# A fused Nyström attention and MLP on one core: batch 0's attention rebuilt step by step, paired x tiles, and the order of the steps written out

## The chip, the cores and the metric

The kernel runs on one core of a Trainium2 chip. The time is device microseconds of one execution, and of several executions the median is given. The core has five engines that run side by side and wait for one another by semaphores: TensorE (PE, with its weight loads listed apart as PEld), VectorE (DVE), ScalarE (ACT), GpSimd (POOL) and SyncE (SP, which issues the DMAs).

## The reference

q, k and v are [8 batches, 8 heads, 576 positions, 64], x has 512 channels, the hidden layer 2048.

```python
q_lm = q.reshape(B, H, 32, 18, D).mean(axis=3)      # 32 landmarks, k_lm likewise
A, Bm, C = sm(q, k_lm), sm(q_lm, k_lm), sm(q_lm, k) # softmax(scale * a @ b.T)
Z = Bm.T / (norm1(Bm) * norminf(Bm) + 1e-6)
for _ in range(6):
    Z = 2 * Z - Z @ Bm @ Z
x = (A @ Z @ C @ v).transpose(0, 2, 1, 3).reshape(B, S, 512)
xn = (x - mean(x)) / sqrt(var(x) + 1e-6) * g_ln
out = x + relu(xn @ w_ch1) @ w_ch2
```

## The kernel before, in words

**Attention.** A batch has two units of four heads (u = 0, 1). For each the kernel loads q, k and v, casts them to fp16 (`nat`), turns them over (`xT`), sums them to landmarks (`lm`), and forms the three exponentials: `psb` (landmarks by landmarks), `psc` (by k, into `ect`) and `psa` (q by landmarks, into `ea`). The softmax of `psb` (`softmax_of`, L756, with `rsum` and `rcr`) and its gram matrix (`gram_of`, L797, with `csum` and `cinv`) give the start `st` of the inverse. `iterate` (L817) is one of six steps: eight 32x32 products on PE into a bank, then one scalar_tensor_tensor on DVE that writes the new `st`. Between the steps stand other matmuls: `pscv`, the product of `ect` with v, whose scaled copy is `cv`, and `psd`, the divisors of `ea`, from which ACT makes `lns`. After the last step, `pszt` and `pszc` are the products of the inverse with `cv`, and `zt` and `zcbd` their copies. `ea` is multiplied by `lns`.

**First layer.** x isn't multiplied by w1. For each batch, m = zt·w1 is formed instead (`products`, `copies`), in four quarters f of 512 columns, and a chunk (128 of the 2048 hidden columns, 16 to a batch) is `psh` = m·ea: eight matmuls of 288 columns, then relu to `hT`. w1 is scaled by g when it comes (`scale_w1`, by POOL or ACT). The mean of x is taken out by the column means of w1: four matmuls per quarter with the constant `lesser` (`less_mean`, L1393), copied to `less` by `copy_mean`; `copies` adds less times `zsum` to m. Later `center_w1` takes the mean out of w1 itself.

**Second layer and x.** x itself comes block by block, 36 blocks of 128 positions, as zcbd·ea, into tiles `xblk` (twelve of [128, 512] in `xpool`); `two_rows` (L857) makes two blocks at once in `psr` and evicts each in two copies of 256 columns. `measure` takes mean and deviation of a block (`six`, `stats`). The second layer is 128x512 matmuls of hT with w2; for late batches some are replaced by seven products of sums (`w2mix`). `finish_block` scales by the deviation, adds x, and the block is stored.

**The order.** `attention0` (L610) is batch 0's attention, a generator written by hand: each `yield` is a point at which the code below `warm(27, 160)` (L1917, the start of the program) issues other work, such as the eight loads of w1 and thirteen of its scales on POOL. `first_layer0` (L1520) is batch 0's first layer with the column means of the quarters 1 to 3 (the mean of quarter 1 before the first chunk, of 2 and 3 after the chunks 2 and 5, the products of a quarter after the chunks 1, 4 and 7). The other batches go in sets (1), (2), (3, 4), (5, 6), (7) through `Coming` (loads, casts, transposes) and `attention2`. From then on `run` (L1888) chooses at every step among five streams: attentions, landmark totals, first layers, batch 0's first rows, second layers. A model, `Clock` (L85), keeps what each engine will be free at; a stream comes next when its operands are there by that model, in the order of the streams, and a table `AFTER` holds some steps back until another stream has come so far. Before each choice `help_out` (L1761) issues the steps beside the streams where an engine is free by the model: loads, casts, jobs of DVE's transposes, measures, centring, mixing of w2. Idle matmuls on zeros (`warm`) stand at the start (27 of 160 columns), after three of the four turned tiles of batch 0 (3 of 256 each) and twice in the softmax and gram (4 and 2 of 256).

The copies of m for one quarter, which the prediction speaks of (before, in `copies`):

```python
n = 2 if (self.b, f) == (0, 0) else 1
for part in range(n):
    cols = ts(part, 512 // n)
    for u, (_, total) in enumerate(self.units):
        dve.scalar_tensor_tensor(out=self.m16[f][:, u, cols], in0=less(f)[:, cols], scalar=total, ...)
    while between:
        between.pop(0)()
```

## Time and profile before

| what | value |
|---|---|
| median of 3 runs | 263.51 us (263.14 to 263.57) |
| span of the profiled execution | 261.4 us |
| PE busy | 252.8 us (97%) |
| DVE, ACT, POOL busy | 209.9, 171.8, 136.8 us |
| moved by DMA | 46.68 MB, of which read 36.70 |
| median before less span | 2.1 us |

The profile is of one execution; its span runs from its first to its last instruction, and what lies around that is in the time of a run. A row of a timeline gives start, duration, engine, line, operation, the written and the read tiles, a count of neighbours put together (then the duration is from the first's start to the last's end), and in brackets the idle time before it with what ended it. In a table by stretches each engine has its busy time with its count of instructions, then follow the granted clock of PE (1.00 is full), the share of the DMA engines and GB/s. Groups give count, total busy time, mean ns of one. Since a helper records each operation, nearly all rows have the helper's line, L312 or L318, and are told apart by tiles.

### The profile page before, as it was taken

Reading aid. Unit: us, or ns where it says so; the run is one execution under the profiler, and the core shown is the slowest. Engines: PE = TensorE matmul, PEld = TensorE weight load, DVE = VectorE, ACT = ScalarE, POOL = GpSimd, SP = SyncE. Lnnn points to the kernel's source line nnn. Section 1 sums busy time; section 2 is a strip of 40 time slices with the busy share of each in tenths; the row PEclk is TensorE's granted clock in tenths of the full one; section 3 lists DMA queues with packets and bytes.
Section 4 is the critical chain, followed back from the end, with each engine's and each line's share of the span. In section 5 each row is a group of like instructions: output and inputs, shape, how many; then the busy total and the mean of one; then the engine's idle time right before and its main releaser. Section 6 shows DMA issues by size and latency. Waiting matters only on the chain.

```text
span 261.4 us, 8559 instructions
## 1 busy us (share of the span) xinstructions
PE 252.8 (97%) x3519; PEld 167.7 (64%) x3519; DVE 209.9 (80%) x480; ACT 171.8 (66%) x332; POOL 136.8 (52%) x162
## 2 busy tenths in 40 slices
PE   7899999999999999999999999999999999999994
PEld 6645754556455574546655466588878875888883
DVE  2767965999979997899996972999399889696862
ACT  2588986458956878489986669634977863766000
POOL 5288779999951889899899955400000014000000
PEclk9999999999999999999999999999999999999999
DMA  6999999999947998669731101110330007100705
GB/s 238 381 393 381 384 391 387 355 251 345 349 145 213 282 375 308 185 158 336 244 84 43 26 21 40 45 38 3 80 84 4 3 11 162 32 3 0 163 19 182
DMA packets 24142, 46.68 MB, mean 179 GB/s; under 512 B 2980, under 2 KB 3240, under 8 KB 24104
## 3 DMA queue, kind: packets, MB, share of 16 engines
q1 hardware_dynamic: 23624, 45.50, 54.5%
q10 hardware_dynamic: 480, 0.66, 0.7%
q8 instruction: 27, 0.44, 0.7%
q14 instruction: 11, 0.09, 0.1%
HBM read 36.70 MB, written 9.44 MB: 177 GB/s over the span
## 4 chain that ended last, share of the span: by engine, by line
PE 82%; DVE 11%; DMA 3%; ACT 2%; issue 1%; SPq 0%; DVEq 0%
PE bank L318 53%; PE psh L318 21%; DMA stg<-in_q_dram 3%; DVE m L312 2%; PE psd L318 2%; PE pscv L318 2%; DVE six L312 1%; DVE xblk L312 1%; DVE w L312 1%; DVE part L312 1%; ACT hT L312 1%; PE psea L318 1%; DVE nat L312 1%; DVE xT L312 1%; PE psec L318 1%
## 5 line engine op out<-in xcount | busy, mean ns | idle before, releaser
L318 PE MATMUL bank<-w,hT 128*128 128x512 f16 (+3 forms) x528 | 109.5, 335 | 0.0
L312 ACT ACTIVATE hT<-psh 128x576 f16<-128x576 f32 x123 | 76.7, 655 | 23.9 <-PE psh L318 22.2
L318 PE MATMUL psh<-ea,m 128*128 128x288 f16 x512 | 79.0, 286 | 0.4 <-DVE ea L312 0.3
L318 PEld LDWEIGHTS <-hT 128*128 128x128 f16 x656 | 60.3, 98 | 29.5 <-issue 4.7
L318 PEld LDWEIGHTS <-m 128*128 128x128 f16 x512 | 49.4, 98 | 19.3 <-issue 2.8
L312 DVE SCALAR_TENSOR_TENSOR xblk<-bank,rstd,xblk 128x256 f32<-128x256 f32 (+2 forms) x77 | 39.2, 543 | 14.8 <-PE bank L318 14.6
L312 POOL TENSOR_TENSOR ea<-ea,lns 128x576 f16<-128x576 f16 x14 | 18.2, 1318 | 53.1 <-ACT lns L312 51.8
L312 POOL CAST nat<-stg 128x1152 f16<-128x1152 f32 x23 | 26.1, 1147 | 11.3 <-DVE xT L312 8.7
L312 DVE BATCH_NORM_STATS2 six<-xblk 128x6 f32<-128x512 f32 x36 | 24.3, 674 | 0.6 <-ACT xblk L312 0.5
L312 POOL CAST natv<-stg 128x1152 f16<-128x1152 f32 (+1 forms) x17 | 19.4, 1166 | 9.4 <-DMA stg<-in_v_dram 7.9
L312 DVE STREAM_TRANSPOSE xT<-nat 128x576 uint32<-128x576 uint32 x28 | 21.2, 759 | 0.0
L318 PE MATMUL bank<-w2mix,hT 128*128 128x256 f16 x128 | 17.7, 273 | 0.0
L318 PE MATMUL bank<-w2mix 128*128 128x256 f16 x128 | 17.4, 273 | 0.0
L312 DVE SCALAR_TENSOR_TENSOR st<-st,bank 128x128 f16<-128x128 f16 (+3 forms) x36 | 13.2, 366 | 5.0 <-PE bank L318 4.8
L312 ACT ACTIVATE lns<-psd 128x576 f32<-128x576 f32 x16 | 10.3, 645 | 7.9 <-PE psd L318 7.7
L312 DVE TENSOR_REDUCE part<-xT 128x32 f16<-128x576 f16 x20 | 14.3, 744 | 0.1
L312 ACT COPY xblk<-bank 128x512 f32<-128x512 f32 (+1 forms) x19 | 11.0, 592 | 4.9 <-PE bank L318 4.8
L312 POOL TENSOR_TENSOR asum<-asum 128x256 f32<-128x256 f32 (+1 forms) x20 | 13.0, 650 | 1.6
L318 PEld LDWEIGHTS <-w2mix 128*128 128x128 f16 x128 | 12.3, 98 | 2.0
L312 ACT ACTIVATE ec<-psec 128x256 f16<-128x256 f32 (+1 forms) x42 | 12.0, 430 | 1.9 <-PE psec L318 1.8
L318 PEld LDWEIGHTS <-st 32*32 32x32 f16 (+1 forms) x380 | 6.5, 90 | 10.5 <-DVE st L312 6.3
L312 POOL TENSOR_TENSOR asum<-nat 128x512 f32<-128x512 f16 x10 | 11.7, 1172 | 1.1 <-ACT nat L312 0.4
(133 smaller groups left out, 375.2 us busy)
## 6 DMA issues: line engine op xcount, KB each, us to landing
stg<-in_q_dram SPq DMA_DIRECT2D x16, 576.0 KB, 6.7
stg<-in_k_dram SPq DMA_DIRECT2D x15, 576.0 KB, 6.0
out_dram<-xblk SPq DMA_DIRECT2D x66, 128.0 KB, 2.4
wstg<-in_moe_w_ch_dram SPq DMA_DIRECT2D x16, 512.0 KB, 7.2
stg<-in_v_dram SPq DMA_DIRECT2D x5, 576.0 KB, 7.7
stg<-in_v_dram SPq DMA_DIRECT2D x40, 72.0 KB, 2.8
stg<-in_v_dram SPq DMA_DIRECT2D x6, 288.0 KB, 5.7
stg<-in_v_dram SPq DMA_DIRECT2D x12, 144.0 KB, 3.1
```

The source lines that it names most:

```text
L312: return lambda *args, **kw: keep(getattr(self.engine, op)(*args, **kw))
L318: keep(nc.tensor.matmul(o, l, r, start=start, stop=stop, tile_position=(rb, cb), skip_group_check=(skip or cb != 0)))
```

## The change

In batch 0: the last k tile is cast in two halves with another order of axes; its turned tile goes partly to a bank and is copied in 512 and 640 columns, the second behind the softmax; the idle matmuls in softmax and gram go, the others become 11 of 384 at the start and 2 of 384 after each of three tiles; the gram has a tile of its own; scores and the divisors are issued unit by unit between the steps; `pscv` is one tile of PSUM's second ring with both units, scaled by one product, one reciprocal and one product; the first quarter's mean is taken after the steps; the `ea` halves 0 go to POOL; `zt` is copied by DVE, unit by unit; the products of the first quarter are issued unit by unit; m comes in 128, 128 and 256 columns for the first quarter and 256 and 256 for the second; `less` comes in 128 and 384. The mean of quarter 1 comes after chunk 1, and the later means and products one chunk later than before. w1's first quarter comes in four DMAs instead of two. Four scales of w1 stand on POOL ahead of the `ea` halves and nine behind.

In all batches: `xpool` holds five pairs [128, 2, 512] and two singles `xone`; `two_rows` evicts in two copies of 512, each on DVE or ACT, whichever the model has free sooner. The choice of the next step, `help_out` and `AFTER` give way to a string `ORDER` that lists the steps: a digit is a stream, a letter a step beside them (J a job, M measure, C centre, X and W mixing, K cast, L load), a number behind it a count. A step that cannot be issued yet is kept in `late` and tried before the next. (The code for sets in `BY_HEAD` and `PAIRED` is added too; both sets are empty.)

```diff
+            for r in range(2) if (nm, u) == ("k", U - 1) else (None,):
...
+                    dve.tensor_copy(out=t[:, :, r, :].rearrange("p j (a d) -> p a j d", a=2),
+                                    in_=raw[nm, u][:, r, :, :].rearrange("p j (a d) -> p a j d", a=2))
...
-    xpool = Ring(name="xpool", bufs=12)
+    xpool = Ring(name="xpool", bufs=5)
...
-        dve.tensor_copy(out=last_tile[0][:], in_=last_tile[1][:])
-        yield "landmarks"
+        t, pst, rest, turn = last_turn
+        dve.tensor_copy(out=t[:, 0:NFIRST, :], in_=pst[:, 0:NFIRST, :])
...
-        st, bmT = softmax_of(psb, W)
-        warm(4, 256)
...
-        cinv, _ = gram_of(p1([P, 4, W * LM], "psse"), st, bmT, W, lambda: warm(2, 256))
...
+        scores_of_q(0)
+        turn(range(NBEFORE, NJ))
+        scores_of_k(0)
+        st, bmT = softmax_of(psb, W)
+        dve.tensor_copy(out=t[:, NFIRST:NJ, :], in_=rest)
+        banks.release(*last_bank)
+        lns = []
+        _, csum = gram_of(p1([P, 4, W * LM], "psse"), st, bmT, W, None, p1([P, 4, W * LM], "gram"))
+        scores_of_q(1)
+        scaled_by_pe()
...
+            if it == 0:
+                scores_of_k(1)
             if it == 1:
+                lns.append(divisors(ea[0]))
+            if it == 2:
                 product(range(NJ // 2))
-            if it == 2:
+            if it == 3:
                 product(range(NJ // 2, NJ))
...
+                dve.tensor_tensor(out=rcv[:], in0=pscv_[0][:, :, D], in1=csum[:], op=ALU.mult)
+                dve.reciprocal(out=rcv[:], in_=rcv[:])
...
+            if it == 4:
+                dve.tensor_tensor(out=cv[:], in0=pscv_[0][:, :, 0:D2],
+                                  in1=rcv[:, :, None].broadcast_to([P, W, D2]), op=ALU.mult)
+                lns.append(divisors(ea[1]))
             if it == 5:
-                less_mean(0, 3, 4, False)
-                scale_ea(0, 0)
+                less_mean(0, 0, 2)
+                scale_ea(dve, 0, 1)
...
+        scale_ea(pool, 0, 0)
+        scale_ea(pool, 1, 0)
...
+        less_mean(0, 2, 4, False)
+        for w in range(W):
+            dve.tensor_copy(out=zt[:, :, w, :], in_=pszt[w][:, :, 0:LM])
+        copy_mean(0)
...
-            copy = sooner(1024, clock.at(t))
-            for i, (j, _) in enumerate(mine):
-                for hp in range(2):
-                    copy(crossed(x_of(j), hp), to[:, hp, i, :, :].rearrange("p u (r d) -> p u r d", r=2))
+            for hp in range(2):
+                sooner(512, clock.at(t))(
+                    crossed(x, hp), to[:, hp, :, :, :].rearrange("p i u (r d) -> p i u r d", r=2))
...
+            for cols in (((ds(0, P), ds(P, P), ds(2 * P, 2 * P)), (ds(0, 256), ds(256, 256)))[f] if self.b == 0 and f < 2
+                         else (ds(0, 512),)):
...
-        less_mean(1)
...
-            if m in (2, 5):
-                f = 2 if m == 2 else 3
+            if m in (1, 3, 6):
+                f = (m + 3) // 3
...
-            if m in (1, 4, 7):
+            if m in (2, 5, 8):
...
+    ORDER = (
+        "2 3 4 215 3 23 M 2 J2 3 22 J3 2 1 3 2 M 22 L J 0 J 2 J 12 L 22 L 1 3 2 0 3 0 43 M 22 "
...
+        for k in order + [None] * 400:
+            settle()
+            late = [x for x in late if not issue(x)]
...
+            elif k in late or not issue(k):
+                late.append(k)
...
-    warm(27, 160)
+    warm(11, 384)
...
-            warm(3, 256)
+            warm(2, 384)
...
     for i in range(8):
         load_w1(i)
+        if i < 2:
+            for c in range(2):
+                scale_w1(i, c, pool)
+    for it in range(7):
+        next(a0)
+    for i in range(2, 8):
         for c in range(2):
-            if i % 2 == 0 or c == 0 or i == 1:
+            if i % 2 == 0 or c == 0:
                 scale_w1(i, c, pool)
```

## The prediction

> **What bounds the kernel now.** I read the page first (busy shares, slices, chain), then the stretches, then the timelines of the opening 25 us, and last the groups by shape.

> ```profile
> PE 252.8 (97%) x3519; PEld 167.7 (64%) x3519; DVE 209.9 (80%) x480; ACT 171.8 (66%) x332; POOL 136.8 (52%) x162
> ...
> PE   7899999999999999999999999999999999999994
> ...
> PEclk9999999999999999999999999999999999999999
> ...
> PE 82%; DVE 11%; DMA 3%; ACT 2%; issue 1%; SPq 0%; DVEq 0%
> ```

> TensorE is busy 97% of 261.4 us and carries 82% of the chain. Only the first two slices and the last show it short of work. So the change can save in two ways: close what is left idle on PE, nearly all of it in the opening, or take away matmul work. The stretches say where the idle time lies (first pair after the stretch: its length and PE's busy time; third: DVE's; then the clock).

> ```profile
> 11.70:14.50 2.80, 2.72 (x77) 1.73 (x77) 2.19 (x9) 1.75 (x4) 2.17 (x2) 1.00 1.01 365
> 18.50:21.40 2.90, 2.28 (x40) 0.98 (x40) 2.54 (x7) 1.95 (x5) 2.78 (x4) 1.00 1.05 386
> 21.40:46.00 24.60, 23.91 (x364) 14.15 (x363) 17.82 (x48) 20.43 (x44) 20.38 (x21) 1.00 1.05 386
> 46.00:70.00 24.00, 23.83 (x241) 13.48 (x245) 23.59 (x48) 16.73 (x33) 22.97 (x25) 1.00 1.00 325
> 70.00:160.00 90.00, 89.82 (x1401) 51.60 (x1374) 78.42 (x173) 68.58 (x137) 71.73 (x74) 1.00 0.61 185
> 160.00:240.00 80.00, 79.94 (x1067) 61.18 (x1065) 64.99 (x149) 54.24 (x103) 9.20 (x7) 1.00 0.16 38
> ```

> PE idles 0.69 us between 21.4 and 46, 0.17 to 70, 0.18 to 160 and 0.06 to 240: 1.1 in all that better cover could close (besides what hides inside the modelled ends of pipelined matmuls). The opening is another matter: 0.62 of the 2.90 from 18.5 on are idle, and before that, "busy" is not useful work: until 18.5 us the 32x32 products and idle matmuls only sit beside a chain of short DVE steps. What sets that stretch is DVE's latency, one step after the other:

> ```profile
> 8.41 2.23 DVE L312 CAST nat<-stg 128x1152 f16<-128x1152 f32 x3 [1.26 <-DMA stg<-in_q_dram]
> ...
> 11.68 0.76 DVE L312 COPY xT<-pst 128x1152 f16<-128x1152 f16 x1 [0.21 <-PE pst L322]
> ...
> 12.43 0.22 DVE L312 TENSOR_REDUCE rsum<-bank 128x2 f32<-128x64 f32 x1
> ...
> 13.80 0.22 DVE L312 TENSOR_REDUCE csum<-bank 128x2 f32<-128x64 f32 x1 [0.42 <-PE bank L318]
> ...
> 14.83 0.29 DVE L312 SCALAR_TENSOR_TENSOR st<-st,bank 128x128 f16<-128x128 f16 x1 [0.35 <-PE bank L318]
> 15.48 0.29 DVE L312 SCALAR_TENSOR_TENSOR st<-st,bank 128x128 f16<-128x128 f16 x1 [0.36 <-PE bank L318]
> ...
> 18.12 0.22 DVE L312 SCALAR_TENSOR_TENSOR st<-st,bank 128x64 f16<-128x64 f16 x1
> ```

> ```profile
> 14.54 0.24 PE L318 MATMUL bank<-st 32*32 32x64 f16 x8
> ...
> 19.67 1.18 PE L318 MATMUL bank<-w,lesser 128*128 128x512 f16 x4
> 20.69 0.41 PE L318 MATMUL psh<-ea,m 128*128 128x288 f16 x2
> 21.38 1.14 PE L318 MATMUL psh<-ea,m 128*128 128x288 f16 x6 [0.28 <-DVE ea L312]
> ```

> The first inverse product starts at 14.54, the last st step ends at 18.34, the first chunk of the first layer (psh) starts at 20.69, and PE runs full from 21.38. From there on an earlier start moves everything behind it, if nothing else is late.

> **The change part by part.** I make the sum against the profiled execution (span 261.4 us; the three timed runs have a median of 263.51, so 2.1 us lie around the span and I leave them unchanged).

> (1) k's last tile is cast in two halves with the short axis outermost. The group rows of the casts, and the transfers of the halves:

> ```profile
> L312 DVE CAST nat<-stg 128x1152 f16<-128x1152 f32 x3 | 2.3, 760 | 5.2 <-DMA stg<-in_q_dram 4.5 <-DMA stg<-in_k_dram 0.7
> ...
> L312 DVE CAST nat<-stg 128x576 f16<-128x576 f32 x2 | 1.5, 754 | 0.0
> ```

> ```profile
> L337 SPq DMA_DIRECT2D stg<-in_k_dram x2: 447/457/467, 2.3 to 2.8; - x2
> ...
> DMA to landing us min/median/max: 6.8/6.9/7.0
> ```

> A half (576) costs as much as a whole (1152): 0.754 against 0.760. The whole walks its two slots outermost, the half its nine. Written as the whole is, a half would take half the whole plus some fixed cost, about 0.40 (my choice); the other bound is the old 0.754, no gain. The second half lands at 2.83 + 7.0 = 9.85 and its cast ends at 10.64 today, so it ends at about 10.29: −0.35. [...]

> (2) Softmax and gram. Today the 0.76 copy of xT stands ahead of rsum, and csum (13.80) waits on PE, where scores and idle matmuls stand ahead of the gram. After: the copy is 512 + 640 with the second behind the softmax, the idle matmuls there go, g's transpose and psc(1) move back, the gram has its own tile. The stages rsum (ready 0.2 sooner without the copy), csum (0.42 of waiting, most of it gone) and (1) add up to −0.9; psa(0), three turns and psc(0) now stand ahead of rsum's products on PE, and I give back 0.15. First inverse product: 14.54 − 0.75 = 13.8 (bounds 13.4 to 14.5, all or nothing).

> (3) The six steps, 0.65 apart (14.83 to 15.48). The same products and exponentials lie between them. New is the scaling of pscv for both units in one operation:

> ```profile
> 16.52 0.23 DVE L312 RECIPROCAL rcv<-bank 128x1 f32<-128x1 f32 x2
> ...
> 16.96 0.41 DVE L312 TENSOR_SCALAR cv<-bank,rcv,cinv 128x130 f16<-128x130 f32 x1
> ```

> ```profile
> L312 DVE TENSOR_TENSOR cv<-pscv,rcv 128x260 f16<-128x260 f32 x3 | 1.3, 428 | 0.1
> ...
> L312 DVE TENSOR_TENSOR rcv<-pscv,csum 128x2 f32<-128x2 f32 x3 | 0.5, 155 | 1.1 <-PE pscv L318 1.1
> ```

> 0.43 replaces 2 x 0.41, but rcv costs 0.16 + 0.17 (product, then reciprocal) where 0.23 was, and the one cv must end before pszt. I charge 0.15: last st ends at 18.34 − 0.75 + 0.15 = 17.75.

> (4) From there to psh. zt goes to DVE, unit by unit; the product of unit 0 comes first; m is written in 128, 128 and 256 columns instead of 256 and 256, `less` in 128 and 384. The chunk's first matmul needs only the first 128 columns of both units, so one m piece of a shorter size, not two of 0.44:

> ```profile
> 19.72 0.88 DVE L312 SCALAR_TENSOR_TENSOR m<-less,zsum,bank 128x256 f16<-128x256 f16 x2
> 20.51 1.19 DVE L312 TENSOR_TENSOR ea<-ea,lns 128x288 f16<-128x288 f16 x2
> ```

> Of four ea halves DVE keeps two (0.54 each by its group); two go to POOL, ahead of nine of its w1 scales. That takes DVE's 1.19 out from between m and psh. First psh: 20.69 − 0.6 − 0.4 = 19.7; the second half of chunk 0, which waits for ea today at 21.38, at about 20.1.

> (5) What is given back. Today's gap isn't empty: the four `lesser` matmuls of w1's second quarter (the row at 19.67) fill it. After the change they follow chunk 1, and two of the first quarter's move out from between the steps to behind pszc. A row of four such matmuls in a full stretch, and a step beside it:

> ```profile
> 40.74 0.24 PE L318 MATMUL bank<-st 32*32 32x64 f16 x8 [0.25 <-DVE st L312]
> 40.91 1.04 PE L318 MATMUL bank<-w,hT 128*128 128x512 f16 x4
> ```

> At about 0.22 each (four, with the last one's tail, in 1.04) the mean's four are 0.9 of work that PE must now do after 20.1, where it used to be free; the first quarter's two still fall into idle time, at most half. So the lead of 1.0 at psh (20.69 to 19.7), and of 1.3 at the second half of chunk 0, shrinks to about 1.3 − 0.9 = **0.4** once chunk 1, that mean and the second product are done. Bounds: −1.0 (the mean's matmuls too find idle time) to 0.

> (6) POOL. Its thirteen w1 scales run unbroken today:

> ```profile
> 16.25 6.60 POOL L312 TENSOR_SCALAR w<-wstg,g_sb 128x512 f16<-128x512 f32 x8 [0.28 <-DMA wstg<-in_moe_w_ch_dram]
> 23.05 2.04 POOL L312 TENSOR_SCALAR w<-wstg,g_sb 128x512 f16<-128x512 f32 x3 [0.21 <-DMA wstg<-in_moe_w_ch_dram]
> 25.84 1.14 POOL L312 CAST nat<-stg 128x1152 f16<-128x1152 f32 x1 [0.75 <-DMA stg<-in_k_dram]
> ```

> After four of them it now waits for unit 1's divisors, whose last exponential is

> ```profile
> 17.77 0.69 ACT L312 ACTIVATE lns<-lns 128x576 f32<-128x576 f32 x1
> ```

> and ends at 18.46 today (about the same after: a step later in the order, 0.6 sooner by (2) and (3)). Then come two ea halves; no row has one on POOL, the nearest are 0.54 on DVE (above) and half of POOL's 1.32 for the whole, so some 0.7 each with DVE's as the lower bound:

> ```profile
> L312 POOL TENSOR_TENSOR ea<-ea,lns 128x576 f16<-128x576 f16 x14 | 18.2, 1318 | 53.1 <-ACT lns L312 51.8
> ```

> The nine scales that follow take 7.4 (6.60 / 8 each; the last three, at 0.68, less) and end at 18.5 + 1.4 + 6.9 = 26 to 27.3 at worst, where the last one ends at 25.09 today; POOL's cast of batch 1's k at 25.84 had 0.75 to spare, so it is 0.2 to 1.5 late. Behind it on POOL stand the three other casts of batch 1, and for them PE's sums and DVE's transposes; but PE has first-layer chunks in plenty there. The second quarter of w1 has two scales on POOL ahead of the mean after chunk 1 (21 to 21.8); they end by 18.5 + 1.4 + 1.6 = 21.5. I cost both at 0; if that cover is gone, PE stands up to 0.6 at that mean, and as much at batch 1's sums.

> (7) SP: two transfers of 512 KB become four of 256, two issues more of 0.457 each (the row of L337), behind the loads of v. Hidden: the queue then waits for stg slots anyway.

> (8) The written order. In batch 1 the softmax now has zcbd's products beside it and st's first wait (0.25 at 40.74) goes, which can give back up to the 0.69 idle of 21.4 to 46; but two inverse steps come together with nothing between, as do pszc and the products, where today matmuls stand. A bare step costs at most its 0.65, less the filler that is then done elsewhere. I take **0** (bounds −0.4 to +0.6). In batch 2 a `center` no longer stands ahead of st on DVE and two matmuls more lie between the steps; in batches 5 and 6 the first step has two matmuls of 512 columns beside it where it had five. By 0.22 a matmul that is 0.4 of cover where 0.65 are needed, some 0.2 lost, and batch 2's gain is the 0.18 idle of its stretch at most: **0** together (bounds ±0.2). The order may close some of the rest of the 1.1: **−0.2** (bounds −0.5 to 0).

> (9) Paired x tiles: 20 copies of 256 columns become 5 of 512 on DVE and seven more on ACT.

> ```profile
> L312 DVE COPY xblk<-psr 128x256 f32<-128x256 f32 x20 | 7.1, 417 | 0.0
> ...
> L312 DVE COPY xblk<-bank 128x512 f32<-128x512 f32 x4 | 2.7, 682 | 0.2 <-PE bank L318 0.2
> ```

> Two of 0.68 for four of 0.42: 0.3 of DVE a time, six times, plus the split over two engines. PE is full there (0.06 idle in 80 us), so little of it reaches the end: **−0.2** (bounds 0 to −0.5), out of what the modelled ends hide. A pair comes free only when both its blocks are stored; five pairs and two singles hold as many blocks as twelve singles did, and the pair reused belongs to a batch stored long ago. Cost 0.

> Matmul work proper: idle matmuls 27 x 160 + 15 x 256 become 17 x 384, in time that waits on transfers anyway. Cost 0.

> Sum: −0.4 (opening) + 0 + 0 − 0.2 (order) − 0.2 (x) = **−0.8**: span 260.6, time 263.5 − 0.8 = **262.7**.

> **The rivals.**

> A, the lead is given back (263.4). For it: DVE is busy 23.59 of 24.00 between 46 and 70 us; if DVE, not PE, sets that stretch, an earlier start of PE is lost there unless DVE starts earlier as well. POOL's 22.97 of 24.00 says the same, and by (6) POOL starts later. Against it: PE is at 23.83, and DVE's own opening ends sooner too. Of the sum only half of (9) is left: −0.1.

> B, slower (264.5). The mechanism is one: inverse steps without cover. Each step is 0.65 of latency (14.83 to 15.48); where the written order puts less than that between two of them, PE stands for the difference. The two bare places of batch 1 (0.65 + 0.4) and two of 0.2 in each of the other four sets make 2.65; less the waits closed (0.7), the opening's 0.4, the order's 0.2 and x's 0.2, it is about +1.0 with 0.15 rounded off. It decides from 0.4 us of missing fill per place on. Against it: those fillers are in the order somewhere, and most places have them.

> C, more is won (261.5). The whole lead of 1.0 at psh survives, because the displaced `lesser` matmuls find idle time, half of the 1.1 of waits goes, and (9) gives its 0.5: −2.0.

> D, the clock (265.2). The granted clock is 1.00 in every stretch. With fewer idle matmuls and no fill in softmax, it may drop between 12 and 20 us: some 3.4 us at half speed are 1.7 lost. [...] No row here shows a drop, and PE has real matmuls in every microsecond of that stretch.

> **How the numbers follow.** Forecast 0.46 (its own range 262.0 to 263.2), A 0.22, B 0.17, C 0.12, D 0.03. 0.2% of 263.5 is 0.53 us, about what a measurement of this kernel can tell from no change: faster is under 262.98, slower over 264.04. Faster: 0.40 of the forecast, all of C, 0.06 of A: 0.58. Slower: B but for 0.02, D, 0.02 of A: 0.20. The rest, 0.22, is the same. Range: C at its end to most of B: **261.2 to 264.4**; below lies half of C's spread, above the rest of B and D.

> **What would show it.** Half casts of 0.40 (1); first inverse product at 13.8 (2); last st step ended by 17.75 (3); first psh near 19.7, PE full from about 20.1 (4); products of chunk 5 about 0.4 sooner (5); POOL's cast of batch 1 at 25.8 to 26.3 (6); in batch 1, PE waits on st of up to 0.4 where two steps adjoin (8); psr copies of 0.68 on DVE (9). The forecast is wrong if PE's idle time in 20 to 70 us grows by more than 0.4, or if the middle (70 to 240) gets shorter by more than 0.5, where I see nothing to win.

## The result, and the profile after

The changed kernel takes 265.48 us (median of 4 runs, 265.22 to 266.1), the kernel before 263.32 (263.04 to 263.57): a ratio of 1.008 with a 95% interval of 1.0063 to 1.0097. The forecast was 262.7 in a range of 261.2 to 264.4. The kernel is slower by 2.2 us where a gain of 0.8 was foretold.

The page of the changed kernel (busy shares, then the slices of PE and of its clock, the code's DMA queue, the chain):

```profile
PE 252.8 (96%) x3494; PEld 166.1 (63%) x3494; DVE 203.5 (77%) x467; ACT 175.0 (66%) x334; POOL 139.9 (53%) x166
...
PE   7869999999999999999999999999999999999994
...
PEclk9995999999999999999999999999999999999999
...
q8 instruction: 27, 0.44, 0.7%
...
PE 89%; DVE 3%; DMA 2%; ACT 2%; issue 2%; SPq 0%; DVEq 0%; ACTq 0%
```

One digit tells most of it: the fourth slice of the clock is a 5 where before had a 9. In the chain "issue" grew from 1% to 2%. DVE's part fell from 11% to 3%, but that alone doesn't show a shorter latency: e9 below, with the same steps, has DVE at 13%. What shows it is the first inverse product, at 13.33 us instead of 14.54. The same stretches as before (length and PE's busy time, then the other engines, the clock ahead of the last two columns):

```profile
14.50:18.50 4.00, 2.06 (x63) 1.12 (x62) 1.18 (x7) 1.50 (x4) 2.75 (x5) 1.00 1.05 399
18.50:21.40 2.90, 2.60 (x44) 0.66 (x44) 1.61 (x7) 2.06 (x5) 1.53 (x3) 0.60 1.08 394
21.40:46.00 24.60, 23.54 (x314) 13.94 (x318) 16.87 (x45) 18.62 (x39) 19.75 (x22) 0.91 1.00 358
46.00:70.00 24.00, 23.58 (x261) 13.70 (x256) 21.86 (x47) 16.30 (x29) 22.67 (x23) 1.00 0.93 311
```

From 14.5 to 18.5 us PE is busy half the time, and by the trace's record of the granted clock it runs at 0.50 from 19.1 to 25.9 us. Its timeline shows what stopped it:

```profile
13.33 0.24 PE L322 MATMUL bank<-st 32*32 32x64 f16 x8 [0.30 <-DVE st L316]
...
15.41 0.42 PE L322 MATMUL pscv<-natv,ect 64*64 64x130 f16 x13
17.56 0.31 PE L322 MATMUL pscv<-natv,ect 64*64 64x130 f16 x7 [1.74 <-issue]
...
18.66 0.66 PE L322 MATMUL bank<-w,lesser 128*128 128x512 f16 x2
...
21.63 2.12 PE L322 MATMUL psh<-ea,m 128*128 128x288 f16 x8 [0.51 <-DVE m L316]
23.54 1.91 PE L322 MATMUL bank<-w,lesser 128*128 128x512 f16 x4
```

PE stands for 1.74 us in the middle of a group of 20 matmuls that all read tiles long written. Nothing of the program holds it; "issue" means that the profile shows no wait. At that point PE has run some 448 instructions (loads and matmuls, by the count of its records). The DMA packets of the queue q8 are 16,384 bytes each, 27 in all for PE's 3494 matmuls and as many loads (259 a packet), so I take them for PE's own code. The first of them starts at 15.25 us of the span and has landed at 16.30; PE goes on 1.26 later. In the kernel before it lands at 14.14, and the 449th instruction starts without a pause at 15.84. After the standstill, matmuls of 512 columns take twice as long (x4 in 1.91 at 23.54, 1.03 before).

To see where time goes over the whole span I compare the two traces at equal work: the sum of matmul columns done, each by the share of the array that it fills, idle matmuls left out. The lead or lag against before, at the times of before:

```
time in before (us)         15    20    25    43   107   119   240
changed kernel           -0.6  +2.2  +3.2  +3.5  +2.3  +2.4  +2.2
e9  (code sooner)         0.0  +0.1  -0.3   0.0  -1.2  -0.1  -0.3
e15 (e9 once more)       -0.4  +1.5  +2.6  +3.0  +1.8  +3.3  +3.1
e16 (late code, idle)    +0.1  +3.3  +3.1  +3.4  +3.0  +3.8  +3.6
e18 (e13 once more)      -0.1  +0.1  -0.2  +0.2  -1.1  -1.0  -1.2
```

Ahead by 0.6 at 15 us, the changed kernel is 3.2 behind at 25; between 43 and 107 us it wins 1.2 back, and from there nothing moves.

### The profile page after: what moved, and what is told of

The parts are those of the page before. It is cut to its first block, busy times and chain, and to the rows that moved or that the text cites. A ratio compares the mean times of both kernels' runs of the same rounds, so it can differ in the third digit from the quotient of the medians.

```text
span 263.6 us, 8510 instructions
## 1 busy us (share of the span) xinstructions
PE 252.8 (96%) x3494; PEld 166.1 (63%) x3494; DVE 203.5 (77%) x467; ACT 175.0 (66%) x334; POOL 139.9 (53%) x166
## 4 chain that ended last, share of the span: by engine, by line
PE 89%; DVE 3%; DMA 2%; ACT 2%; issue 2%; SPq 0%; DVEq 0%; ACTq 0%
PE bank L322 57%; PE psh L322 23%; DMA stg<-in_q_dram 2%; PE pscv L322 2%; PE psd L322 1%; PE psec L322 1%; ACT hT L316 1%; PE psea L322 1%; DVE w2mix L316 1%; ACT xblk L316 1%; PE psr L322 1%; PE pszt L322 1%; DVE st L316 0%; DVE zcbd L316 0%; DVE xblk L316 0%
## 5 line engine op out<-in xcount | busy, mean ns | idle before, releaser
L322 PE MATMUL bank<-w,hT 128*128 128x512 f16 (+3 forms) x528 | 111.1, 334 | 0.2 <-DVE xblk L316 0.2
L316 ACT ACTIVATE hT<-psh 128x576 f16<-128x576 f32 x123 | 78.0, 654 | 20.3 <-PE psh L322 18.5
L322 PE MATMUL psh<-ea,m 128*128 128x288 f16 x512 | 81.9, 289 | 0.6 <-DVE m L316 0.5
L322 PEld LDWEIGHTS <-hT 128*128 128x128 f16 x656 | 60.7, 98 | 29.3 <-issue 4.6
L322 PEld LDWEIGHTS <-m 128*128 128x128 f16 x512 | 49.7, 99 | 21.3 <-issue 2.0
L316 DVE SCALAR_TENSOR_TENSOR xblk<-bank,rstd,xblk 128x256 f32<-128x256 f32 (+2 forms) x77 | 38.9, 538 | 14.3 <-PE bank L322 14.2
L316 POOL TENSOR_TENSOR ea<-ea,lns 128x576 f16<-128x576 f16 (+1 forms) x16 | 19.7, 1242 | 54.7 <-PE bank L322 46.5
L316 POOL CAST nat<-stg 128x1152 f16<-128x1152 f32 x25 | 28.9, 1172 | 9.1 <-DVE xT L316 6.9
L322 PE MATMUL bank<-w2mix,hT 128*128 128x256 f16 x128 | 17.4, 273 | 0.0
L322 PE MATMUL bank<-w2mix 128*128 128x256 f16 x128 | 17.1, 273 | 0.0
L316 DVE TENSOR_REDUCE part<-xT 128x32 f16<-128x576 f16 x20 | 14.5, 743 | 0.1
L316 ACT COPY xblk<-bank 128x512 f32<-128x512 f32 (+1 forms) x20 | 12.0, 600 | 3.7 <-PE bank L322 3.2
L322 PEld LDWEIGHTS <-w2mix 128*128 128x128 f16 x128 | 12.4, 98 | 1.9
L322 PEld LDWEIGHTS <-st 32*32 32x32 f16 (+1 forms) x380 | 6.7, 90 | 10.5 <-DVE st L316 5.1
L316 ACT CAST m<-bank 128x512 f16<-128x512 f32 x17 | 9.8, 589 | 4.4 <-PE bank L322 3.5
```

The costliest lines, as they stand in the source:

```text
L316: return lambda *args, **kw: keep(getattr(self.engine, op)(*args, **kw))
L322: keep(nc.tensor.matmul(o, l, r, start=start, stop=stop, tile_position=(rb, cb), skip_group_check=(skip or cb != 0)))
```

## The experiments

**Theory Q**, later F: PE runs out of fetched code, because the packet stands in the DMA queues behind data; the clock falls after the standstill. **Rival I**: the clock falls because idle work was taken out; the standstill is beside the point. **Rival H**: the written order loses what the opening wins. (The times of packets and of first psh in the expectations are 0.3 us later than the span's; those in my text are the span's.)

**e1: w1's first quarter in two DMAs again.**

```diff
-        if f == 0:
+        if False:
             parted[stg.name] = DM
```

> The changed kernel with one part undone: w1's first quarter comes in two DMAs of 512 KB, as before, instead of four of 256. [...] Rival I (the clock drops because the idle matmuls and fillers are gone; the standstill is a matter of chance or of something else): 265.5 us, clock 0.987, standstill as before. Rival N (the code is late, but not because of the small transfers): the code's start within 0.5 us of 15.5, 265 to 266 us.

265.32 us, ratio 1.0082 (1.0054 to 1.0109), clock 0.987, packet at 14.9, standstill 1.0. By theory Q the packet would have come near the 13.2 of before and PE would not have stood. The small transfers are at most a part of it (the packet is 0.35 sooner, the standstill 0.7 shorter): rival N holds. All eight executions lost clock (0.986 to 0.992).

**e2: the kernel before with the four small DMAs.** The edit is the added branch of `load_w1` alone.

> The kernel before with that one part alone: w1's first quarter in four DMAs of 256 KB. Theory Q: the code's packet starts 1 to 2 us later than the 13.5 us of before; the kernel before has about 1.7 us to spare there, so a standstill of 0 to 1 us and, if it is long enough, a lower clock: 263.5 to 266. Rivals I and N: 263.3 within 0.3, clock 1.00.

264.85, ratio 1.005 (1.0027 to 1.0073), but the packet comes at 13.26 as in before and PE doesn't stand at 16 us. The planner, fed with other transfers, moved steps elsewhere, and the loss lies in batch 2's inverse steps (PE's timeline, then two stretches):

```profile
76.88 0.31 PE L318 MATMUL bank<-st 128*128 128x160 f16 x2 [0.52 <-DVE st L312]
77.78 0.31 PE L318 MATMUL bank<-st 128*128 128x160 f16 x2 [0.58 <-DVE st L312]
78.67 0.31 PE L318 MATMUL bank<-st 128*128 128x160 f16 x2 [0.58 <-DVE st L312]
```

```profile
77.00:80.00 3.00, 1.83 (x19) 1.33 (x18) 1.95 (x4) 0.00 (x0) 0.91 (x1) 0.86 0.73 207
80.00:83.00 3.00, 3.00 (x34) 0.96 (x33) 1.51 (x4) 0.29 (x2) 0.00 (x0) 0.57 0.72 207
```

Three steps without cover (my rival B's mechanism) cost their 1.7 us, and in the profiled execution and two more of ten the clock as well (0.991 or 0.992; the seven others have 0.997 or more and take 264.5 to 265.0). So e2 refutes theory Q's part on the small transfers, and its time says nothing of them.

**e3, e4: more instructions at the start; more idle work in the steps.**

```diff
-    warm(11, 384)
+    warm(33, 128)          # e3
...
+            if it in (0, 1, 2):
+                warm(1, 384)  # e4
```

> The changed kernel with 33 idle matmuls of 128 columns at the start instead of 11 of 384: the same PE time, 44 instructions (loads and matmuls) more. [...] Theory Q: the code is asked for sooner, in front of more of the w1 transfers; the standstill shrinks by about 1 us or goes: 262 to 264.5 us. Rival I: the same standstill and clock drop or a longer one, 265.5 us or more.

> The changed kernel with one idle matmul of 384 columns more after each of the inverse steps 0, 1 and 2, in time that PE stands there anyway. Theory Q with a clock that falls because of the standstill of 1.7 us: standstill stays (within 0.5 us) and the clock still falls to 0.5 for some 7 us: 265 to 266 us. Rival I (the missing idle work decides the clock): the standstill stays, the clock stays at 1.00, 262 to 263 us.

e3: packet at 13.0, no standstill, clock 0.999, first psh at 19.07; yet 265.71 (ratio 1.0076, 1.0054 to 1.0098). Its planner saw other times and moved instructions of DVE and ACT: at 102.79 us PE waits 1.33 for st. The opening did as theory Q said, the time did not; four of its ten executions lost clock (0.981 to 0.994). e4: 265.76 (1.0061 to 1.0119); the profiled execution has a standstill of 1.3 and the clock at 0.987, as in the changed kernel. But three of its ten executions kept the clock (0.999 or more) and took 264.55 to 264.79, where the changed kernel's four all lost it (0.981 to 0.987). So rival I's idle work helps at times, and the full clock alone does not bring the time back.

From here on the planner is told of the old idle matmuls, so that the other engines' instructions stay in the compared kernel's order.

**e5 to e8: the number of instructions ahead of the code's request.**

```diff
-    warm(11, 384)
+    idle_as(27, 160, 11, 384)   # e5: 27 of 160 run, the planner told of 11 of 384
...
-    warm(27, 160)
+    idle_as(11, 384, 27, 160)   # e6: the kernel before
...
# e7: e5 with each eviction of 512 columns as two of 256
# e8: e5 with lead, help_out, AFTER and run of before in place of ORDER
```

> The changed kernel with 27 idle matmuls of 160 columns at the start, as before, instead of 11 of 384: the same PE time, 32 instructions more ahead of everything; the planner is told of the old ones, so that every other engine's order is the changed kernel's. Theory F (code waits in line behind the data transfers issued ahead of its request; the request comes when TensorE has run some 100 instructions; with 32 instructions fewer at the start it comes 1.7 us later, behind more of w1): TensorE's first code packet starts near 13.5 us instead of 15.5, no standstill, clock 1.00 throughout without any other idle work, first psh near 19.1 us, 261 to 262.3 us. Rival G (the code's wait depends on the order of the rest or on chance): packet at 15 us or later, standstill, 265 us. Rival H (no standstill, yet the written order loses what the opening gains): no standstill, 263 to 264.5 us.

> The kernel before with 11 idle matmuls of 384 columns at its start instead of 27 of 160, the rest untouched. Theory F: its first code packet starts 1.5 to 2 us later than 13.5 us; TensorE needs it at about 16.5 us, so it stands some 0 to 1 us and, if the clock follows, loses up to 3 us more: 263.8 to 266.5 us. Rivals G and H: 263.3 within 0.3, packet at 13.5 us.

> As e5_idle_count, with one part undone: each psr tile is evicted in four copies of 256 columns instead of two of 512, on the engine that the planner picked. If the paired evictions are worth the 0.2 us that I forecast: e5 + 0.2 (within 0.1 to 0.5). If they are worth nothing: e5 within 0.1.

> As e5_idle_count, with one part undone: the next step is chosen by before's model and table (its counts of the first layer's steps moved by the four that batch 0 has more) instead of the written order. If the written order closes waits between 40 and 90 us, as the changed kernel's trace says (its loss against before falls from 3.6 to 2.4 us there): e5 + 0.8 to 1.5 us. If rival H is right and the written order costs time: e5 - 0.5 or less.

e5: 266.23 (ratio 1.0069 to 1.0135), packet at 14.7, standstill 1.3: 32 instructions more were not enough. e6: 263.88 (1.0006 to 1.0056); packet at 14.97 instead of 13.2. The kernel before, with nothing but fewer idle matmuls, gets the standstill (its row among PE's waits) and in the profiled execution loses the clock too (two stretches); of its ten executions four lost clock (0.987 to 0.994), and the other six took 263.53 to 263.88:

```profile
PE bank L318 <- issue: 1.1, 1, 1.1
```

```profile
15.00:18.00 3.00, 1.90 (x63) 1.16 (x62) 0.81 (x5) 1.54 (x3) 2.49 (x5) 0.89 1.03 390
18.00:21.00 3.00, 3.00 (x46) 0.84 (x46) 1.83 (x7) 1.33 (x2) 2.34 (x4) 0.54 1.05 388
```

e7 266.87, e8 267.55 (each of 4 runs): e8 against e5 is +1.3 as expected, against rival H; e7 against e5 is +0.6, with both spreads over 2 us wide.

By now the packets fall in two groups, and with e9 to e18 it stays so. The time of PE's 138th instruction, by the span, against the start of the first packet: 7.6 to 8.4 us and 13.0 to 13.6 (before, e2, e3, e9 to e12, e14, e15, e17); 9.0 to 10.0 us and 14.7 to 15.3 (the changed kernel, e1, e4 to e8, e16); 5.9 and 6.3 us and 10.65 (e13, e18). Between the two first groups w1's next transfers are issued. No trace shows the request itself; I infer that it comes near the 138th instruction, and that the packet then waits 4.4 to 5.9 us behind what SP has issued. The count is narrow because PE pauses: when it goes idle near 8 us (in e5 from 7.7 to 9.1), e5, e7 and e8 have run 136 instructions, and their code is late; before and e14 have run 140, and theirs is not. That is why e5's 32 were not enough.

**e9 to e11: the code sooner, all else untouched.**

```diff
-    warm(11, 384)
+    idle_as(33, 128, 11, 384)   # e9; e10 with e7's evictions, e11 with e8's chooser
```

> The changed kernel with 33 idle matmuls of 128 columns at the start instead of 11 of 384, as in e3_more_code_early, but with the planner told of the old ones, so that all other instructions stand exactly as in the changed kernel. Theory F (the first code packet waits behind the w1 transfers that are issued before its request; that request comes after some 136 to 139 instructions, by the packets of the eight kernels so far): request at about 8.2 us, packet starts at 13.3 us, no standstill of TensorE at 16 us, clock at least 0.995, first psh at 19.1 us instead of 21.6; of the 2.2 us lost the standstill (1.7) and the half clock (7 us at 0.5) are won back, less what TensorE idled there anyway: 261 to 262.5 us, below the kernel before. Rival H (the written order loses what the opening gains, as e3's time of 265.7 could be read): no standstill, 264.5 us or more.

> As e9_more_code_only with the psr evictions in four copies of 256 columns instead of two of 512. My forecast of the paired evictions: e9 + 0.2 (within 0.1 to 0.5); e7 against e5 had + 0.6 with wide spread.

> As e9_more_code_only with before's model and table choosing the steps instead of the written order. By e8 against e5: e9 + 1.3 us (within 0.7 to 2). If rival H holds, below e9.

e9: 263.69, ratio 1.0 (0.9973 to 1.0026), 12 runs from 261.62 to 265.89; the profiled one 262.9 with clock 0.999 and no standstill, but five of the twelve lost clock (0.981 to 0.993). e11: 265.43 (1.0052 to 1.0126), again against rival H. e10: 262.73, ratio 0.9968 (0.995 to 0.9985), the only version measured clear of the kernel before; not what I expected, and its profiled run lost its clock with 0.30 us of standstill only (three stretches):

```profile
12.00:15.00 3.00, 2.47 (x76) 1.46 (x69) 2.01 (x9) 2.23 (x5) 2.32 (x3) 1.00 1.00 335
15.00:18.00 3.00, 2.70 (x71) 1.43 (x64) 1.43 (x7) 1.40 (x3) 2.43 (x4) 0.63 1.06 407
18.00:21.00 3.00, 2.70 (x36) 0.43 (x34) 1.37 (x6) 1.96 (x5) 2.06 (x4) 0.50 1.06 389
```

Part of e10's lead over e9 is the clock, which only two of its ten executions lost: where it was kept, e10 has a median of 262.5 (262.07 to 263.34) and e9 of 263.0 (261.62 to 265.12).

Theory F had to be widened: late code is one cause, and light work in the new opening may be another (**theory L**, against **S**: standstills alone).

**e12 to e15: idle work back in the opening.**

```diff
# e12: e9, and unseen by the planner
+    idle_more(2, 256)   # in the gram, and again ahead of the first step
...
+            if it < 5:
+                idle_more(1, 256)
# e13: the same, with idle_as(60, 64, 11, 384) at the start
# e14: before, idle matmuls in softmax and gram 32 columns wide instead of 256
```

> e9_more_code_only with nine idle matmuls of 256 columns more, unseen by the planner: two in the gram, two ahead of the first inverse product, one after each of the steps 0 to 4. Theory L (the clock falls when TensorE has done little work in the opening, be it by a standstill or by 32x32 products alone; the code packet and the light work are two separate causes): clock 1.00 in the profile and few or no slow executions, 261.3 to 262.8 us with a spread as small as before's. Theory S (the clock falls after standstills alone): as e9, 263.7 us with its wide spread. Should the 18 instructions bring the code's end too near (TensorE resumes about 1 us after the packet has landed, with 0 to 0.2 us to spare in e9 and e10): a standstill of 0.3 to 0.6 us that the idle work should outweigh.

> As e12_code_and_idle, with 60 idle matmuls of 64 columns at the start instead of 33 of 128 (about the same PE time, 54 instructions more): the request for code falls near 6 us, ahead of nearly all of w1; its packet starts near 12.0 us, and the code runs out some 1.4 us sooner than in e9, at 14.2 to 14.5. Theory L with the line of transfers: no standstill or one under 0.3 us, clock 1.00, 261.3 to 262.8 us. If the request is answered no sooner (13.3 us): a standstill of about 1 us and 263 to 265 us.

> The kernel before with the six idle matmuls in its softmax and gram cut from 256 columns to 32: the same instructions, less work. Theory L: the clock falls in some or all executions, 263.5 to 266 us with a wider spread. Theory S: no standstill, so 263.3 within 0.3 and clock 1.00.

> e9_more_code_only once more, one look at the clock. Theory L: it varies from execution to execution with nothing else changed (0.98 to 1.00 on average), and the time with it, 261.6 to 266 us.

e15 is the same program as e9. It took 266.33 with the clock at 0.981, where e9's profiled run took 262.9 at 0.999. Neither has a standstill for code. Three stretches of e9, then of e15:

```profile
12.00:15.00 3.00, 2.52 (x76) 1.63 (x73) 2.13 (x11) 2.23 (x4) 2.80 (x4) 1.00 0.97 348
15.00:18.00 3.00, 2.87 (x98) 1.38 (x96) 2.10 (x9) 2.34 (x5) 2.40 (x4) 1.00 1.05 402
18.00:21.00 3.00, 2.50 (x40) 0.89 (x34) 2.76 (x10) 2.21 (x5) 2.55 (x5) 1.00 1.06 387
```

```profile
12.00:15.00 3.00, 2.47 (x73) 1.43 (x71) 1.92 (x9) 2.23 (x5) 2.80 (x4) 1.00 0.99 342
15.00:18.00 3.00, 2.87 (x68) 1.38 (x64) 1.71 (x8) 1.58 (x3) 2.19 (x4) 0.57 1.05 406
18.00:21.00 3.00, 2.48 (x37) 0.50 (x35) 1.33 (x6) 1.96 (x5) 2.04 (x3) 0.50 1.05 384
```

By its record e15's clock falls at 15.39 us. PE is "busy" about as long in both ahead of that (2.52 and 2.47 of 3) and after it, and only one has half the clock: theory S falls. e12: 263.55, ratio 1.0003 (0.9977 to 1.0029); e13: 263.28, 0.9996 (0.9981 to 1.0011), its 12 runs within 262.75 to 264.06; both profiles with the clock at 1.0. (In two of e12's twelve it was 0.992 and 0.994; in e13's never under 0.998.) e14: 263.33, 0.9995 (0.9984 to 1.0005), clock 1.0: taking that idle work from the kernel before costs nothing, against theory L's expectation. Before has full 512-column `lesser` matmuls between its steps 3 to 5, which the change moved behind them; so it is not the six idle matmuls alone that keep its clock. Whether those keep it wasn't tried.

**e16 to e18.** e16 is the changed kernel with e12's nine idle matmuls and its own late code; e17 and e18 are e12 and e13 once more.

> The changed kernel with the nine idle matmuls of e12 in its gram and steps and its own 11 of 384 at the start, so that the code comes as late as in the changed kernel. If the clock falls for want of work over a window and the standstill of about 1.7 us is part of that: the clock falls all the same, 264.5 to 266 us. If the nine idle matmuls outweigh the standstill: clock 1.00, the standstill costs its own 1 to 1.7 us and no more, 263.8 to 265 us.

> e12_code_and_idle once more, one look at the clock. If the idle work holds it: 1.00 again and 262.5 to 264.2 us; if e12's was luck, as e9's against e15's: 0.98 to 0.99 and 265 to 266.5 us.

> e13_code_first once more, one look at the clock. If the idle work holds it: 1.00 again and 262.7 to 264.1 us; otherwise 0.98 to 0.99 and 265 us or more.

e16: 265.9 (ratio 1.005 to 1.0117), standstill 1.3, and the clock falls all the same, for 3.41 us instead of 6.83 (two stretches):

```profile
15.00:18.00 3.00, 1.69 (x55) 0.98 (x54) 0.82 (x3) 1.54 (x3) 2.47 (x4) 1.00 1.05 396
18.00:21.00 3.00, 3.00 (x61) 1.14 (x53) 1.75 (x8) 1.33 (x2) 0.32 (x1) 0.59 1.05 387
```

e17: 262.8, with 0.21 us of standstill; e18: 262.14, both with the clock at 1.00. Over all timed executions the mean clock was under 0.996 in none of 107 of the kernel before and in 4 of 4 of the changed kernel; with late code in 4 of 4 of e16 and 4 of 10 of e6; with light work in 5 of 12 of e9 and 2 of 10 of e10; with both mended in 2 of 12 of e12 and none of 12 of e13. So late code by itself can take the clock, and so can light work.

**What the falls have in common.** In all twenty traces the record of the granted clock changes only in whole steps of 3.41 us (in the changed kernel's it is full for 13.65 us, half for 6.83 and full again for 238.93: 4, 2 and 70 steps). I cut each trace into these steps and added up the matmul columns that start in each, weighted by the share of the array as in the table above, but with the idle matmuls (the busiest steps have some 8,300). These steps stand just ahead of the falls in the opening (start in us, columns), and these are the emptiest ones there after which the clock stayed full:

```
fell    changed 15.67 1875   e1 13.63 2222   e4 15.64 2208   e5 12.70 2076   e6 13.93 2000
        e7 12.20 2220   e8 13.57 1788   e10 12.36 2039   e15 11.98 2167   e16 15.12 1778
stayed  before 12.85 3394   changed 12.26 2526   e9 11.61 2640   e11 12.49 2746
        e3 12.98 3058   e14 13.86 3154   e12 12.18 3736   e13 12.80 3624
```

Over the whole traces 1,452 steps at full clock were followed by another, and none of them had fewer than 2,526 columns. The one fall that doesn't fit is e2's at 79 us, after 2,880. So for the clock a standstill and light work are one cause: each leaves a step with too little in it. In e7 the clock even falls at 15.62, ahead of its standstill (15.76 to 17.33). And e9 against e15 is luck: one program, but the step begins 0.37 us later in e15 and holds 2,167 columns instead of 2,640. I worked this out after the runs; none was made to test it.

## Why the prediction was wrong

- **The step that failed** is "Matmul work proper: idle matmuls 27 x 160 + 15 x 256 become 17 x 384, in time that waits on transfers anyway. Cost 0." I counted them as time only. They are also instructions: ahead of PE's pause near 8 us there are 36 fewer (104 against 140: 16 matmuls and loads at the start, 2 after the turned tiles), so PE's 138th comes at 9.5 us instead of 7.9, and by the account above the code is asked for behind more of w1 and comes later than its use. They are also part of the work that keeps the clock (five of e9's twelve executions lost it, two of e12's, with nine idle matmuls more), with the `lesser` matmuls that the change moved (e14 shows that the six in softmax and gram alone do not decide it). Standstill and half clock together put the changed kernel 3.2 us behind at 25 us of the span, where e9 is 0.3 ahead.
- **Rival D** named the clock, priced it at 1.7 us and gave it 0.03. Its reason against, "PE has real matmuls in every microsecond of that stretch", is refuted by e15: its clock fell though PE was shown busy for 2.86 of the 3.41 us ahead, in part with 32x32 products (2,167 columns in all). When the rival was written no row showed the 3.4 us at half speed in its sum; e6 and e16 then showed 3.41 us at 0.50. In the changed kernel the half clock lasted twice the 3.4 us that the rival took, 6.8 (19.1 to 25.9); in e15, where it lasted 10.2, it alone put 2.9 us between e15 and e9, the same program, at 25 us. The standstill of 1.74 the rival did not foresee. The changed kernel has both and is 3.5 behind e9 there; how much of that is each one's is not shown.
- DVE's groups by shape in the changed kernel have the two durations that I had bounded for (1) and (9):

```profile
L316 DVE CAST nat<-stg 128x576 f16<-128x576 f32 x2 | 0.9, 460 | 0.3 <-DMA stg<-in_k_dram 0.3
...
L316 DVE COPY xblk<-psr 128x512 f32<-128x512 f32 x5 | 3.4, 679 | 0.0
```

- **(1) to (4) were right, (2) to (4) too small.** A half cast takes 0.46 (forecast 0.40; 0.754 in before, with the axes in the other order; why the order counts no run shows). The first inverse product starts at 13.33 (13.8). Where code and clock hold (e3), the last st ends at 17.19 (17.75) and psh starts at 19.07 (19.7).
- **(5) was right in size.** I let a lead of 1.3 shrink to 0.4; at equal work e9 leads by 0.3 at 25 us and e18 by 0.2, and nothing is left at 43. Both signs of being wrong came: PE's idle time from 21.4 to 70 us grew by 0.6 (0.86 to 1.48), and by equal work the changed kernel wins 0.6 between 70 and 240.
- **(6)** POOL's first cast of batch 1 came at 26.75 (25.8 to 27.3), and no wait for it shows on PE.
- **(8) was mis-sized.** Against before the changed kernel wins 1.2 us between 43 and 107 us (forecast 0.2 over all), and e11, with before's chooser, ends 1.7 behind e9 by the medians, so the order is worth more than I gave it. In batch 1 the written order pays what (8) gave as its bound: PE waits 0.40 for st at 44.66 us, and 0.40 for hT at 38.42 (before: 0.25 and 0.27, both for st):

```profile
PE bank L322 <- DVE st L316: 0.7, 2, 0.4
...
PE psec L322 <- ACT hT L316: 0.4, 1, 0.4
```

  The order is also tight: in e13 POOL is one sum later than in e18, ACT waits for POOL's ea and PE for ACT's lns at 117 us; e9, e15 and e16 have the same wait (0.7 to 1.0). PE's row for it among the waits of e13:

```profile
PE pszc L322 <- ACT lns L316: 0.7, 1, 0.7
```

- **(9) is worth nothing that I can see.** The copies take 0.68 on DVE, as forecast; but between 154 and 240 us e9 and e10, with halves and with quarters, gain the same 0.35 and 0.34 on before.
- **Rival A** is what is left by its number, not by its mechanism: with code and clock mended, e12 and e13 are the same as before to within 0.3% (the 95% intervals). But A has the lead lost between 46 and 70 us for want of DVE or POOL; in the runs it is gone by 43, and between 43 and 107 time is won. Single executions (261.62 of e9, 262.14 of e18) are below all 107 of before (262.25 at the least); whether a version with both mended and quarters (as e10's time suggests) beats it for good stays open.

## What to carry to other kernels

Count what an edit does to the number of instructions ahead of a tight place, not only to their time: here the code came by DMA, in packets of 16,384 bytes, and with 36 instructions fewer ahead of PE's pause the first of them started at 15.25 us instead of 13.21, by my inference behind more of the kernel's own transfers. Look in the trace for a group cut in two by an "issue" gap and for the code queue's packets before you blame a semaphore. Idle matmuls and full-width work between tiny products are not slack as long as the clock hangs on them; before taking them out, add up the matmul work by stretches of a few us (here the clock's record has steps of 3.41), and check that the clock stays full in several executions, since the same program can lose it or not (e9's profiled execution had 0.999, e15's 0.981).

## What the runs showed of the hardware

```profile
21.00:24.00 3.00, 3.00 (x11) 1.39 (x12) 2.47 (x8) 1.47 (x3) 3.00 (x6) 0.50 1.03 377
```
